# An adaLN block with linear attention and a gated MLP on one core: the columns of c first, other dummies, another order, the gate row at the joint, the last tile in two parts

## The chip, the core and the metric

The kernel runs on one core of a Trainium2 chip. Times are device microseconds (us) of one execution, and a kernel is judged by the median of several executions. The core has five instruction queues that are named here as in the profile: TensorE (PE, with its weight loads as PEld), VectorE (DVE), ScalarE (ACT), GpSimd (POOL) and SyncE (SP). SyncE only issues DMAs; ScalarE issues some as well.

## The reference

```python
mod = (silu(c) @ w_mod).reshape(c.shape[0], 6, 1, -1)
sa, ca, ga, sb, cb, gb = mod[:, 0], ..., mod[:, 5]
h = layernorm(x) * (1 + ca) + sa
x = x + ga * A(h)            # linear attention, 16 heads of 28
h = layernorm(x) * (1 + cb) + sb
x = x + gb * B(h)            # gated MLP with a spatial matrix
return x

def A(x):
    q, k, v = heads(x @ wqkv)
    phi_q = concat(softmax(q @ w_phi), softmax(-(q @ w_phi)))
    phi_k = concat(softmax(k @ w_phi), softmax(-(k @ w_phi)))
    kv, z = phi_k.T @ v, sum(phi_k)
    return merge((phi_q @ kv) / (phi_q @ z + 1e-6)) @ wo

def B(x):
    z = gelu(x @ w_in)
    z1, z2 = z[..., :896], layernorm(z[..., 896:])
    return (z1 * (w_sp @ z2 + b_sp)) @ w_out
```

x is [1, 2048, 448], c is [1, 448], w_sp is 2048 x 2048, w_in is 448 x 1792; everything is bf16. The six rows of mod depend on c alone.

## The kernel before

The 2048 tokens are 16 tiles of 128. The kernel is one long straight program: a string named ORDER lists some 890 steps, a loop runs through it and calls one small function for each step, and each function issues its instructions on its engine. Nothing is scheduled by a compiler: every engine executes its instructions in the order of the string, and waits at each for what it needs. A step is written `name:arguments@slot/engine`. The slot is the place in PSUM (A0, A1, A2 of two banks, B0, B1 of one) that the step's matmuls write, and a slot can be written again only when the last step that read it is done. The engine is V, S, G or Y for VectorE, ScalarE, GpSimd or SyncE; `ld:wk/Y` is the load of wk issued on SyncE's queue. The same words in another order are another schedule of the same arithmetic.

The steps that are spoken of, in the order of the program:

- `du:8` is eight dummy matmuls of 128x256 on a tile `zero` of zeros (L729, warm_ps). They compute nothing; they keep TensorE at work while the first data come in. `consts` fills `zero` on VectorE (L687).
- `ct` turns the row c into four columns by four tiny TensorE transposes (L740, ct_ps); `ce:1` to `ce:4` make silu of them (L747 to 753; ScalarE, then VectorE). `csA`, `ccA`, `csB`, `ccB` multiply these columns with sections of w_mod (L764, cf_ps, 16 one-column matmuls each); `esA`, `ecA`, `esB`, `ecB` read the products out on VectorE (L768, 771). sa and ca serve the first layer norm, sb and cb the second.
- `l1s`, `l1e`, `l1r`, `l1a` are the first layer norm: bn_stats of a tile on VectorE, moments, reciprocal root, and the normalised tile (L867, into xpad). `X` and `XE` transpose the first four tiles on TensorE (L880, xt_ps) and copy them out; `T1` transposes the others by a DMA on SyncE's queue (L872).
- `FT`, `ET`, `FS`, `PF`, `EP` fold w_phi and the scale into the weights Wk and Wq. `FT` transposes wk or wq.
- `kM`, `vM`, `qM` are the projections (L890, 898, 945), `kE`, `qE` the exponentials on ScalarE (L950 for q), `kS`, `kR`, `kP` the softmax of k, `kA` the accumulation of kv (L921), `KV`, `KZ` its reading. Up to here TensorE works on k and v; then the *joint*: kv is complete, and the stage of the attention's output begins.
- `gr:0` and `gr:1` make the gates ga and gb as 128 equal rows (L956, gr_ps, four matmuls of 448 columns each), `ge` copies them out on ScalarE, `wos` and `wts` multiply them into wo and w_out.
- `nM`, `nX`, `nC`, `nS`, `nT`, `nA`, `T2` are numerator, denominator, division and transpose of the attention's output; `wM` its product with wo (L1005, x_ps); `wR` adds the residual (L1012, f_x).
- `l2R`, `l2r`, `l2a`, `T3` are the second layer norm; `zM`, `zG`, `zQ`, `zR`, `zW`, `zN` the second half of z with its own layer norm (L1049 matmuls, L1017 squares, L1025 to 1035 moments, L1072 the normalised z2n); `yM`, `yG` the first half (L1078).
- `W` transposes w_sp by DMA. `tT`, `sS` form sums of blocks (L1102, L1109) so that seven products of blocks do for eight in w_sp @ z2; `P` are these products (L1124), `d` and `x` put them together (L1133 on VectorE, L1140 on GpSimd), `gM`, `gG` the last 128 columns, done plainly (L1145).
- `oM`, `oE`, `oD` are the output tile: seven matmuls of 448 columns (L1159, o_ps), the residual addition on VectorE (L1162) and the store (L1165).

How the string is read, and the loads on which the prediction speaks:

```python
"c": lambda q: q.dma_start(out=c_row[:], in_=c),
"wk": lambda q: load_rows(q, wk_raw[0:CB, :, 0:D], A_wqkv[:, D:2 * D]),
"win1": lambda q: load_rows(q, win_s[0:CB, 2:4], B_w_in[2 * CB:]),

def du(n, slot):
    wps = bank(slot, "warm_ps")
    for _ in range(n):
        nc.tensor.matmul(wps[:, 0, 0:256], lhsT=zero[:, 0:P], rhs=zero[:, 0:256], start=True, stop=True)
```

## Time and profile before

| what | value |
|---|---|
| runs (us) | 248.95, 249.26, 249.69; median 249.26 |
| profiled execution | 249.4 us, of which the span of the profile is 247.6 |
| instructions | 4188 |
| busy: PE, PEld, DVE, ACT, POOL | 97%, 51%, 74%, 42%, 47% of the span |
| HBM | 8.87 MB read, 1.84 MB written, 43 GB/s over the span |
| largest groups of matmuls | block products L1124 (29% of the chain that ended last), output L1159 (9%), z L1049 (7%) |

The profile is of one execution; times in it count from the start of its span, and 1.8 us of the execution lie outside it. An engine's busy share is the share of the span in which it executes. The chain that ended last is followed back from the last instruction to what released each step. In a row of a timeline, the bracket at the end gives the idle time of the engine just before the row and what ended it.

### The profile page before, as it was taken

The numbers are of one execution on the slowest core, as the hardware profiler recorded it, in microseconds if no ns is written. First come the engines' busy times: TensorE is split into PE (matmuls) and PEld (weight loads), VectorE is DVE, ScalarE is ACT, GpSimd is POOL, SyncE is SP. The second block draws the span as 40 slices with busy tenths as digits, with TensorE's granted clock in tenths as the row PEclk, the third lists the DMA queues.
The fourth block names the chain that finished last, engine by engine and source line by source line (L and its number), as shares of the span: only waits on it lengthen the run. The fifth ranks groups of instructions, "written<-read, shape, count | busy, mean of one in ns | idle before, by whom it ended". The sixth has DMA issues, their size and how long they took to land.

```text
span 247.6 us, 4188 instructions
## 1 busy us (share of the span) xinstructions
PE 240.5 (97%) x1533; PEld 126.8 (51%) x1533; DVE 182.5 (74%) x369; ACT 104.8 (42%) x217; POOL 116.3 (47%) x175
## 2 busy tenths in 40 slices
PE   8999999999999999999999999999999999999992
PEld 5865556675665564444444444444444444444451
DVE  4689998967999989686571997798976363645562
ACT  2488887836999896866897100000000000000000
POOL 3667997500387668987509000521129610124430
PEclk9999999999999999999999999999999999999998
DMA  7973849746235787989990999000001000101022
GB/s 178 293 217 102 193 86 177 194 113 178 51 72 110 127 162 136 163 158 176 179 177 0 162 181 173 0 1 0 3 0 37 0 0 3 56 0 37 21 95 65
DMA packets 68207, 25.22 MB, mean 102 GB/s; under 512 B 58129, under 2 KB 67602, under 8 KB 68178
## 3 DMA queue, kind: packets, MB, share of 16 engines
q1 hardware_dynamic: 66210, 22.57, 46.1%
q10 hardware_dynamic: 1968, 2.29, 3.3%
q8 instruction: 14, 0.23, 0.4%
q14 instruction: 15, 0.12, 0.2%
HBM read 8.87 MB, written 1.84 MB: 43 GB/s over the span
## 4 chain that ended last, share of the span: by engine, by line
PE 85%; POOL 6%; ACT 3%; DVE 2%; DMA 1%; issue 1%; POOLq 0%
PE g_ps L1124 29%; PE o_ps L1159 9%; PE z_ps L1049 7%; PE q_ps L945 6%; PE k_ps L890 5%; PE v_ps L898 5%; PE g_ps L1145 5%; PE z_ps L1078 4%; PE x_ps L1005 4%; PE kvacc L921 3%; PE warm_ps L729 3%; PE num L973 2%; POOL f_zv L1035 1%; DMA f_hT<-f_xpad 1%; DVE f_z2n L1072 1%
## 5 line engine op out<-in xcount | busy, mean ns | idle before, releaser
L1133 DVE TENSOR_TENSOR f_zb<-g_ps,f_zb 128x512 f32<-128x512 f32 (+1 forms) x31 | 20.5, 670 | 17.1 <-PE g_ps L1124 16.7
L1124 PEld LDWEIGHTS <-f_z2n 128*128 128x128 bf16 x192 | 18.8, 98 | 22.7 <-issue 0.3
L1140 POOL TENSOR_TENSOR f_z1T<-f_zb,f_z1T 128x512 bf16<-128x512 f32 (+1 forms) x11 | 12.0, 1102 | 33.6 <-DVE f_zb L1133 33.6
L1049 PE MATMUL z_ps<-f_ar,f_hT 112*128 112x448 bf16 (+1 forms) x128 | 26.6, 352 | 0.0
L1140 POOL TENSOR_TENSOR f_z1T<-f_Sx,f_z1T 128x512 bf16<-128x512 f32 x6 | 8.0, 1332 | 39.3 <-DVE f_Sx L1133 39.3
L1078 PE MATMUL z_ps<-f_hT,f_ar 112*128 112x512 bf16 x112 | 26.1, 379 | 0.0
L1159 PE MATMUL o_ps<-f_wout,f_z1T 128*128 128x448 bf16 x112 | 22.5, 352 | 0.0
L1124 PE MATMUL g_ps<-f_ar 128*128 128x512 bf16 x96 | 22.4, 379 | 0.0
L1081 ACT ACTIVATE f_z1T<-z_ps,f_zb 128x512 bf16<-128x512 f32 x28 | 18.2, 684 | 5.2 <-PE z_ps L1078 5.1
L950 ACT ACTIVATE f_Eq<-q_ps 112x1024 bf16<-112x1024 f32 x16 | 16.3, 1032 | 5.8 <-PE q_ps L945 5.8
L1049 PEld LDWEIGHTS <-f_hT 112*128 112x128 bf16 (+1 forms) x128 | 12.2, 97 | 11.6
L1078 PEld LDWEIGHTS <-f_ar 112*128 112x128 bf16 x112 | 11.0, 98 | 12.6
L893 ACT ACTIVATE f_E<-k_ps 128x448 bf16<-128x448 f32 x32 | 15.8, 555 | 3.8 <-PE k_ps L890 3.7
L989 DVE TENSOR_TENSOR f_ar<-num,f_w 128x896 bf16<-128x896 f32 x16 | 17.0, 1087 | 0.4
L904 DVE TENSOR_REDUCE f_ksum<-f_E 128x32 f32<-128x896 bf16 x16 | 16.9, 1064 | 0.5 <-ACT f_E L893 0.4
L1124 PE MATMUL g_ps<-f_Eq,f_z2n 128*128 128x512 bf16 x72 | 16.5, 379 | 0.0
L1159 PEld LDWEIGHTS <-f_z1T 128*128 128x128 bf16 x112 | 11.0, 98 | 10.7
L1053 ACT ACTIVATE f_zb<-z_ps 128x896 bf16<-128x896 f32 x16 | 14.6, 913 | 4.1 <-PE z_ps L1049 3.8
L1162 DVE TENSOR_TENSOR f_xpad<-o_ps,f_x 128x448 bf16<-128x448 f32 x16 | 9.9, 622 | 8.0 <-PE o_ps L1159 7.9
L945 PE MATMUL q_ps<-f_hT,f_Wq 113*128 113x512 bf16 (+1 forms) x64 | 15.0, 379 | 0.6 <-ACT f_Eq L950 0.6
L1124 PEld LDWEIGHTS <-f_ar 128*128 128x128 bf16 x96 | 9.4, 98 | 11.1 <-DVE f_ar L1102 0.2
L1005 PE MATMUL x_ps<-f_ar 112*128 112x448 bf16 x64 | 14.1, 352 | 0.3 <-DVE f_x L1012 0.3
(202 smaller groups left out, 473.1 us busy)
## 6 DMA issues: line engine op xcount, KB each, us to landing
out_dram<-f_xpad SPq DMA_DIRECT2D x16, 112.0 KB, 1.7
f_wm<-in_w_mod_dram SPq DMA_DIRECT2D x4, 406.0 KB, 5.1
f_x<-in_A_x_dram SPq DMA_DIRECT2D x2, 448.0 KB, 7.8
f_wmg<-in_w_mod_dram SPq DMA_DIRECT2D x2, 392.0 KB, 9.9
f_ar<-in_B_w_in_dram SPq DMA_DIRECT2D x1, 784.0 KB, 5.6
f_ar<-in_B_w_in_dram ACTq DMA_DIRECT2D x1, 784.0 KB, 5.4
f_wout<-in_B_w_out_dram ACTq DMA_DIRECT2D x1, 784.0 KB, 5.6
f_bsp<-in_B_b_sp_dram SPq DMA_DIRECT2D x1, 512.0 KB, 5.7
```

The lines of the kernel that those rows point to most:

```text
L904: nc.vector.tensor_reduce(out=ksum[:, i], in_=Er[i % NR][:].rearrange("p s (c f h) -> p (s c) h f", c=4, h=HP), axis=AX.X, op=ALU.add)
L945: nc.tensor.matmul(t[:, u, :], lhsT=Wq[0:KR[m], m, cc * CB:cc * CB + P], rhs=hT[0:KR[m], 4 * st:4 * st + 4, m, :], start=(m == 0), stop=(m ...
L950: nc.scalar.activation(out=Eq[st // 2][0:CB, 2 * c2:2 * c2 + 2, s, (st % 2) * 512:(st % 2 + 1) * 512], in_=ps["q" + str(n)][0:CB, :, :], f ...
L989: nc.vector.tensor_tensor(out=tr[i % 2][:], in0=numv(i)[:, :, :, 0:DH], in1=wr[i // 2 % 2][:, i % 2].unsqueeze(3).to_broadcast([P, 2, H, D ...
L1005: nc.tensor.matmul(t[:, 0, 0:D], lhsT=oT[0:CB, i % 4, cc, :], rhs=wo_s[0:CB, cc, :], start=(cc == 0 and not with_x), stop=(cc == KC - 1))
L1049: nc.tensor.matmul(t[:, hf, 0:D], lhsT=hT[0:KR[m], i, m, :], rhs=win_s[0:KR[m], m, FH + hf * D:FH + (hf + 1) * D], start=(m == 0), stop=(m ...
L1078: nc.tensor.matmul(t[:, 0, :], lhsT=win_s[0:CB, m, fc * P:(fc + 1) * P], rhs=hT[0:CB, 4 * st:4 * st + 4, m, :], start=(m == 0), stop=(m == ...
L1081: nc.scalar.activation(out=stage_b()["z1T"][:, fc, st * 512:(st + 1) * 512], in_=ps["y%d_%d" % (st, fc)][:, 0, :], func=ACT.Gelu_apprx_tan ...
L1124: nc.tensor.matmul(g, lhsT=sta[:, m, :], rhs=mov[:, m, :], start=(m == 0 and i in (1, 6, 7)), stop=(m == 7), skip_group_check=True)
L1133: nc.vector.tensor_tensor(out=o, in0=x, in1=y, op=ALU.add)
L1140: eng.tensor_tensor(out=z, in0=T[r][:, c0:c1], in1=z, op=ALU.mult)
L1159: nc.tensor.matmul(ps["o" + str(t)][:, 0, 0:D], lhsT=later["z1T"][:, FO[n], t * P:(t + 1) * P], rhs=wout_s[:, FO[n], :], start=(n == 0), s ...
```

## The change

Six edits are made together.

1. The load of c is the first DMA on ScalarE's queue, ahead of x1 and x0. Before, it was the second on SyncE's, behind wk.
2. `zero` is filled in its first 256 columns only, and this fill is VectorE's first instruction; before it was the third, over all 512 columns.
3. The dummies: 8 + 3 + 11 = 22 stood ahead of the columns of c, then 2 between the transposes of wk and 6 behind them. Now 18 stand ahead of the columns, 6 behind them, then the same 2, then 8. `csA` goes ahead of `X:0`.
4. From about the third v projection on the steps stand in another order, and several of them on another engine or slot. Among the loads win1 is now where x5 was on ScalarE's queue.
5. `gr:1` moves from the middle of the k and v projections to the joint, between the columns of cb and sb and the next q projection, into slot B0, and `ecB` (the reading of cb's columns, which stood in B0) ahead of the first `nC`.
6. The last output tile is made in two parts, columns 0 to 255 and 256 to 447, each with its own matmuls, addition and store (the new functions oP, oF, oG); the first store is issued on ScalarE's queue.

The diff, with the table cut to its start, the joint and its end:

```diff
 ORDER = """
-tbl du:8@B1 m2b/V ld:wk/Y du:3@A2 m2a/V du:11@A1 ld:c/Y ct@B0 ld:x1/S l1s:1 ld:x0/S l1s:0 m1/G ld:phi/Y ce:1 m3 FTk:1@B1 ...
-l1e:0,1/G FTk:0@A0 ld:wca/Y ce:3 ce:4 bd/V ld:x2/Y ld:wq/Y l1r:0,1 l1a:0/V du:6@A2 X:0@B0 ETk:0/S csA@A2 ETk:1/V ...
+tbl ld:c/S du:18@A1 m2b/V ld:wk/Y m2a/V ct@B0 ld:x1/S l1s:1 ld:x0/S l1s:0 m1/G ld:phi/Y ce:1 m3 du:6@A0 FTk:1@B1 ...
+l1e:0,1/G FTk:0@A0 ld:wca/Y ce:3 ce:4 bd/V ld:x2/Y ld:wq/Y l1r:0,1 l1a:0/V du:8@A1 csA@A2 X:0@B0 ETk:0/S ETk:1/V ...
...
-... nM:0@A1 qE:3 ld:wout/S nM:1@A0 nX:0 nX:1 qF:3 nC:0 csB@B0 W:0,1 ld:win1/Y nC:1 nS:0 ccB@B1 nT:0 qM:4@A2 qE:4 ...
+... nM:0@A1 nM:1@A0 nX:0 nX:1 ccB@B0 ecB nC:0 nC:1 nS:0 qF:3 nT:0 nA:0/V csB@B1 gr:1@B0 ge:1 qM:4@A2 qF:4 T2:0,1 ...
...
-... oM:14,0,7@B0 oM:15,0,7@B1 oE:14 oD:14/Y oE:15 oD:15/Y
+... oM:14,0,7@B0 oP:15,0,256@B1 oE:14 oD:14/Y oP:15,256,448@B0 oF:15,0,256 oG:15,0,256/S oF:15,256,448 oG:15,256,448/Y
...
     def consts():
+        nc.vector.memset(zero[:, 0:256], 0.0)
         nc.gpsimd.memset(wk_raw[0:CB, :, D:D + 16], 0.0)
         nc.gpsimd.memset(wq_raw[0:CB, :, D:D + 16], 0.0)
         nc.vector.memset(one1[:], 1.0)
         nc.vector.memset(warm[:], 0.0)
-        nc.vector.memset(zero[:], 0.0)
...
+    def oP(t, a, b, slot):
+        o = ps["op" + str(a)] = bank(slot, "o_ps")
+        for n in range(FC):
+            nc.tensor.matmul(o[:, 0, 0:b - a], lhsT=later["z1T"][:, FO[n], t * P:(t + 1) * P], rhs=wout_s[:, FO[n], a:b], start=(n == 0), stop=(n == FC - 1))
+
+    def oF(t, a, b):
+        nc.vector.tensor_tensor(out=later["ot"][t % 4][:, a:b], in0=ps["op" + str(a)][:, 0, 0:b - a], in1=x_sb[:, t, a:b], op=ALU.add)
+
+    def oG(t, a, b, eng):
+        eng.dma_start(out=outv[t][:, a:b], in_=later["ot"][t % 4][:, a:b])
```

What that does to single engines is shown at three places. First SyncE's queue at the program's start, before (f_c_row is the row c, f_wm the sections of w_mod):

```order
L645 DMA f_wk_raw<-in_A_wqkv_dram 112x4x448
L655 DMA f_c_row<-in_c_dram 1x448
L649 DMA f_phi<-in_A_w_phi_dram 112x4x28
L652 DMA f_wm_119<-in_w_mod_dram 112x4x464 x2
L658 DMA f_x<-in_A_x_dram 128x2x448
```

and ScalarE at the start of the changed kernel, where the same load now stands (its lines are 43 lower, since the string is shorter):

```order
L689 ACT_TABLE_LOAD
L689 ACTIVATE f_warm<-f_warm 128x1
L612 DMA f_c_row<-in_c_dram 1x448
L614 DMA f_x<-in_A_x_dram 128x448
L613 DMA f_x<-in_A_x_dram 128x448
L704 ACTIVATE f_e<-ct_ps 112x4
```

The load of c has left SyncE's queue, and x1 and x0 (L614, L613) stand one issue later on ScalarE's.

Second, VectorE at the joint, before (the first two rows read kv out; num is the numerators' PSUM, f_dn the denominators, f_cb the columns of cb):

```order
L931 TENSOR_TENSOR f_ar<-kvacc,f_mask 112x16x29 x2
L936 SCALAR_TENSOR_TENSOR f_ar<-kvacc,f_mask 112x16 x2
L980 TENSOR_TENSOR f_cr_101<-num,f_Sx 128x32 x2
L984 TENSOR_TENSOR f_dn_103<-f_cr_101 128x32
L985 RECIPROCAL f_dn_103<-f_dn_103 128x32
L986 TENSOR_TENSOR f_w_105<-f_Sx,f_dn_103 128x64
L989 TENSOR_TENSOR f_ar<-num,f_w_105 128x896
L995 TENSOR_TENSOR f_ar<-f_ar 128x4x112
L989 TENSOR_TENSOR f_ar<-num,f_w_105 128x896
L768 TENSOR_SCALAR f_cb_83<-cf_ps 112x4
```

and now:

```order
L888 TENSOR_TENSOR f_ar<-kvacc,f_mask 112x16x29 x2
L893 SCALAR_TENSOR_TENSOR f_ar<-kvacc,f_mask 112x16 x2
L725 TENSOR_SCALAR f_cb_83<-cf_ps 112x4
L937 TENSOR_TENSOR f_cr_101<-num,f_Sx 128x32 x2
L941 TENSOR_TENSOR f_dn_103<-f_cr_101 128x32
L942 RECIPROCAL f_dn_103<-f_dn_103 128x32
L943 TENSOR_TENSOR f_w_105<-f_Sx,f_dn_103 128x64
L946 TENSOR_TENSOR f_ar<-num,f_w_105 128x896
L952 TENSOR_TENSOR f_ar<-f_ar 128x4x112
```

The reading of cf_ps has moved from behind the division chain to a place ahead of it. On TensorE this piece is new behind the last column of the joint (gr_ps is gr:1; f_scb holds silu(c) in 128 equal columns, f_wmg the gate sections):

```order
L721 MATMUL cf_ps<-f_scol,f_wm_119 128x1
L913 LDWEIGHTS f_scb
L913 MATMUL gr_ps<-f_wmg,f_scb 128x448
L913 LDWEIGHTS f_scb
L913 MATMUL gr_ps<-f_wmg,f_scb 128x448
L913 LDWEIGHTS f_scb
L913 MATMUL gr_ps<-f_wmg,f_scb 128x448
L913 LDWEIGHTS f_scb
L913 MATMUL gr_ps<-f_wmg,f_scb 128x448
L902 LDWEIGHTS f_Wq
L902 MATMUL q_ps<-f_hT,f_Wq 128x512
```

Before, the columns (L764) were followed at once by the q projection (L945).

Third, VectorE around the residuals of tiles 10, 13 and 12, before (f_z2n is a normalised z2, f_zm and f_zv its moments, x_ps the product with wo):

```order
L1019 SCALAR_TENSOR_TENSOR f_ar,f_zs_93<-f_zb 128x896
L995 TENSOR_TENSOR f_ar<-f_ar 128x4x112
L1012 SCALAR_TENSOR_TENSOR f_x,f_s_88<-x_ps,f_x 128x448 x2
L1025 TENSOR_SCALAR f_zm<-f_zs_92 128x2
L1026 TENSOR_TENSOR f_sq<-f_zm 128x2
L1031 SCALAR_TENSOR_TENSOR f_zv<-f_zs_93,f_sq 128x2
L1032 TENSOR_SCALAR f_zv<-f_zv 128x2
L1072 TENSOR_SCALAR f_z2n<-f_zb,f_zm,f_zv 128x896
L1012 SCALAR_TENSOR_TENSOR f_x,f_s_88<-x_ps,f_x 128x448
```

and the same number of instructions in, now:

```order
L969 SCALAR_TENSOR_TENSOR f_x,f_s_88<-x_ps,f_x 128x448
L946 TENSOR_TENSOR f_ar<-num,f_w_106 128x896
L1029 TENSOR_SCALAR f_z2n<-f_zb,f_zm,f_zv 128x896
L952 TENSOR_TENSOR f_ar<-f_ar 128x4x112 x2
L969 SCALAR_TENSOR_TENSOR f_x,f_s_88<-x_ps,f_x 128x448 x2
L976 SCALAR_TENSOR_TENSOR f_ar,f_s_89<-f_x 128x448
L969 SCALAR_TENSOR_TENSOR f_x,f_s_88<-x_ps,f_x 128x448
```

The moments of z (L1025 to 1032) no longer stand between the residuals of this stretch, and z2n stands at other places among them.

More of the change, by code (lines that the diff above doesn't have):

```diff
@@ L494 @@
-W:0,6 kF:14 kE:15 kA:8@A0 kA:9@A0 kP:12/V kS:14 vM:11@A1 kF:15 kS:15 kA:10@A0 vM:14@B1 kR:14 vC:11 vM:15@B0 vC:14 vM:12@A2 vM:13@B1 vC:12 kA:11@A0 vC:13
-kP:13/G kA:12@A0 kR:15 kP:14/V kP:15/V wos:2/V kA:13@A0 kA:14@A0 vC:15 kA:15@A0 KV:0/V KV:1/V KZ:0 ld:win0/S qM:3@A2 KZ:1 nM:0@A1 qE:3 ld:wout/S nM:1@A0
-nX:0 nX:1 qF:3 nC:0 csB@B0 W:0,1 ld:win1/Y nC:1 nS:0 ccB@B1 nT:0 qM:4@A2 qE:4 nA:0/V nT:1 ecB nA:1/V wos:3/V qM:5@A1 nM:2@A0 qF:4 esB nX:2 nM:3@A2 nX:3
-FB@B1 wos:1/V nC:2 qE:5 T2:0,1 nC:3 nS:1 FBc/S qF:5 nT:2 nA:2/G wM:0/S@B0 nT:3 SHw:3@B1 wR:0/S SCw:0,3/S T2:1,2 nM:5@A1 nX:5 nM:4@A0 nC:5 nX:4 nC:4 nA:3/V
@@ L522 @@
[L522 to L525 removed]
+ORDER = """
@@ L1200, in fast_path @@
         "zM": zM, "zG": zG, "zQ": zQ, "zR": lambda a, b, eng: moments(a, b, eng, zs1, zs2, float(FH), zm, zv), "zW": lambda a, b: rpow(a, b, zv), "zN": zN,
-        "yM": yM, "yG": yG, "W": W, "gM": gM, "gG": gG, "tT": tT, "sS": sS, "gal": gal, "P": pM, "d": pD, "x": pX, "oM": oM, "oE": oE, "oD": oD, "guard": guard, "read": read, "hint": hint,
+        "yM": yM, "yG": yG, "W": W, "gM": gM, "gG": gG, "tT": tT, "sS": sS, "gal": gal, "P": pM, "d": pD, "x": pX, "oM": oM, "oE": oE, "oP": oP, "oF": oF, "oG": oG, "oD": oD, "guard": guard, "read": read, "hint": hint,
     }
```

41 lines of the change are left out of this document (1 added, 40 removed).

## The prediction

> **What bounds the kernel now.** I read the page's first part, then busy time of TensorE alone in stretches cut at its idle places, then the chain that ended last, then the timeline at each place. The first line is the page's; the others are the stretches (us, length, busy and matmuls, granted clock, DMA share, GB/s).
>
> ```profile
> PE 240.5 (97%) x1533; PEld 126.8 (51%) x1533; DVE 182.5 (74%) x369; ACT 104.8 (42%) x217; POOL 116.3 (47%) x175
> ...
> 0.00:1.23 1.23, 0.00 (x0) 1.00 0.00 0
> 1.23:54.00 52.77, 52.48 (x479) 1.00 0.75 172
> 54.00:58.00 4.00, 3.42 (x58) 1.00 0.93 263
> ...
> 243.20:247.59 4.39, 0.00 (x0) 0.78 0.20 63
> ```
>
> TensorE is busy 240.5 of 247.6 us. Of the 7.1 us of idle time 1.23 lie before its first matmul, 0.29 up to 54, 0.58 at the joint of the two stages (54 to 58) and 4.39 behind its last matmul; of the 0.6 that are left, two holes of 0.26 and 0.24 make up most (near 103 and 138, rows below). Nothing else matters unless it lets TensorE start earlier, takes matmuls away, closes one of the holes, opens a new one, or shortens the tail. The chain's rows (start, length, what) show what TensorE does first:
>
> ```profile
> 1.23 4.88 PE warm_ps L729 x22
> 6.11 0.46 PE ct_ps L740 x4
> ...
> 8.04 0.66 PE warm_ps L729 x6
> ...
> 9.55 0.26 PE xt_ps L880 x4
> ...
> 23.49 1.51 PE gr_ps L956 x8
> ```
>
> The dummies (warm_ps) lie on the chain: 22 of them at 4.88 / 22 = 222 ns, and six of them later at 0.66 / 6 = 110 ns. A dummy added here is therefore paid in full, with 0.22 or 0.11 us, unless the matmul behind it would have waited anyway.
>
> **The start.** Rows of the timeline (start, length, engine, line, what; idle time in brackets):
>
> ```profile
> 0.82 0.06 DVE L686 MEMSET f_warm<- 128x1 f32 x1
> ...
> 0.90 0.27 DVE L687 MEMSET f_zero<- 128x256 uint32 x1
> 0.92 0.38 ACTq L657 DMA_DIRECT2D f_x<-in_A_x_dram  x1
> ...
> 6.61 0.17 ACT L747 ACTIVATE f_e<-ct_ps 112x4 f32<-112x4 bf16 x1 [4.39 <-PE ct_ps L740]
> ...
> 8.65 0.71 POOL L867 TENSOR_SCALAR f_xpad<-f_x,f_nm,f_rs 128x448 bf16<-128x448 bf16 x1
> ```
>
> The fill of zero, which the dummies wait for, becomes VectorE's first instruction and half as long: between the 0.06 of a tiny fill and the 0.27 of the whole one, about 0.16. It ends near 0.94 instead of 1.17: **-0.23 us**, as everything behind it starts that much earlier. Eighteen dummies then end at 1.00 + 18 x 0.222 = 5.0, and the columns of c come a good 1.0 us earlier than at 6.11. That by itself gives little: the columns' first reader (0.17 on ScalarE) feeds a VectorE step that stands in the queue behind both bn_stats pairs of x, and what the next dummies and transposes wait for is not c. Behind the columns stand 6 + 2 + 8 dummies where 2 + 6 stood. Ahead of the first transposes of wk there are then 24 where there were 22, and ahead of wsa's columns (cf_ps) 34 where there were 30. Four dummies more cost 4 x 0.11 = 0.44 at the later rate and 4 x 0.222 = 0.89 at the earlier one. The first two fall about where the rate changes, the last two behind it: I take 0.18 + 0.22 = **+0.40**. From below: they cost nothing where TensorE would wait for x instead. x1 and x0 now stand behind c on ScalarE's queue, one issue of 0.38 later, and the second normalised tile, ready at 8.65 + 0.71 = 9.36, would come at up to 9.74, while its transposes (9.55 in the chain) come at about 9.7. So nothing is lost there beyond the dummies. Start and ramp together: +0.17, with ends -0.23 (the dummies free) and +0.66 (all at the earlier rate).
>
> The clock column reads 1.00 in the stretch from 1.23, although the same dummy takes twice as long there as later. [...]
>
> **The gate row at the joint.** gr:1 is four of the eight gr_ps matmuls (1.51 / 2 = 0.76 us). Before, it stands at 23.5 in an unbroken run of TensorE. The rows of the joint:
>
> ```profile
> 55.80 0.94 PE L764 MATMUL cf_ps<-f_scol,f_wm 112*128 112x1 bf16 x32
> ...
> 56.22 1.05 ACT L950 ACTIVATE f_Eq<-q_ps 112x1024 bf16<-112x1024 f32 x1
> ...
> 57.32 3.63 PE L945 MATMUL q_ps<-f_hT,f_Wq 113*128 113x512 bf16 x16 [0.58 <-ACT f_Eq L950]
> ...
> 59.92 0.15 DVE L768 TENSOR_SCALAR f_cb<-cf_ps 112x4 f32<-112x4 f32 x1
> ```
>
> Between the columns (end 56.74) and the next q matmuls (57.32, which need a PSUM slot that the second exponential still reads) TensorE idles 0.58. gr:1 takes 0.76 of work from the full stretch and puts it into this hole; what does not fit is 0.18. Net **-0.58 us**. Its slot B0 held the scale columns, so it must wait for the 0.15 read on VectorE, which stood at 59.92 and now goes ahead of the first nC. It is ready some 0.2 us after the columns of the scale, while the shift columns run. Behind it on VectorE the first division chain starts 0.15 later, which I take as covered: the q matmuls (3.63) stand between it and its reader. ScalarE's copy ge:1 goes behind the second exponential, where nobody waits for it. Ends: 0 (the hole only moves) and -0.58; I take the full value because the hole's length is set by ScalarE, whose two exponentials keep their place.
>
> **The other order.** The same matmuls, with other engines and places. The two late holes and what stood in front:
>
> ```profile
> 102.61 0.51 DVE L1072 TENSOR_SCALAR f_z2n<-f_zb,f_zm,f_zv 128x896 bf16<-128x896 bf16 x1 [1.96 <-POOL f_zv L1035]
> ...
> 103.04 0.62 DVE L1012 SCALAR_TENSOR_TENSOR f_x<-x_ps,f_x 128x448 bf16<-128x448 f32 x1
> ...
> 103.72 0.92 PE L1005 MATMUL x_ps<-f_ar 112*128 112x448 bf16 x4 [0.26 <-DVE f_x L1012]
> ...
> 130.11 2.12 POOL L1102 TENSOR_TENSOR f_ar<-f_z2n 128x1024 bf16<-128x1024 bf16 x1 [7.34 <-ACT f_ar L1017]
> ...
> 135.07 1.71 DVE L1072 TENSOR_SCALAR f_z2n<-f_zb,f_zm,f_zv 128x896 bf16<-128x896 bf16 x2 [6.42 <-POOL f_zv L1035]
> ...
> 137.87 1.04 PE L1145 MATMUL g_ps<-f_Eq,f_z2n 128*128 128x512 bf16 x4 [0.24 <-DVE f_z2n L1072]
> ```
>
> At 103 the residual of tile 10 stood behind a z2n that waited 1.96 us for GpSimd; in the new order it stands ahead of any such z2n. At 138 tile 12's z2n came after a 2.12 us subtraction on GpSimd; the new order gives that subtraction to VectorE, behind gG:1, and tile 12 to GpSimd. I count both holes as closed, **-0.50** (end 0 if each only moves).
>
> What is late next: the new order is as tight as the old. The first place is the transposed tiles 4 and 5 (T1:4,6).
>
> ```profile
> 19.51 0.39 ACTq L661 DMA_DIRECT2D f_x<-in_A_x_dram  x1
> ...
> 22.75 2.73 SPq L872 DMA_TRANSPOSE f_hT<-f_xpad  x2
> ...
> DMA to landing us min/median/max: 3.1/3.2/3.3
> ...
> 26.57 1.68 PE L890 MATMUL k_ps<-f_Wk,f_hT 113*128 113x448 bf16 x8
> ...
> f_ar<-in_B_w_in_dram ACTq DMA_DIRECT2D x1, 784.0 KB, 5.4
> ```
>
> They land at 22.75 + 3.3 = 26.05, and kM:5 reads them at 26.57; without gr:1 and with kA:0 (0.42) ahead of it, it comes at 26.23. That leaves 0.2 us, and win1, 784 KB and 5.4 us to landing, is now issued on ScalarE's queue where x5 (448 KB) was at 19.51, so its tail still moves when they do. A dozen such places have a few tenths to spare; I put **+0.30** for new holes, from 0 to the 1.08 that the old order's holes sum to.
>
> **The last tile.**
>
> ```profile
> 232.58 0.42 DVE L1133 TENSOR_TENSOR f_zb<-g_ps,f_zb 128x256 f32<-128x256 f32 x1 [0.51 <-PE g_ps L1124]
> ...
> 235.77 0.68 DVE L1133 TENSOR_TENSOR f_zb<-g_ps,f_zb 128x512 f32<-128x512 f32 x1
> ...
> 243.17 0.62 DVE L1162 TENSOR_TENSOR f_xpad<-o_ps,f_x 128x448 bf16<-128x448 f32 x1 [0.70 <-PE o_ps L1159]
> 243.83 0.43 SPq L1165 DMA_DIRECT2D out_dram<-f_xpad  x1
> ```
>
> The last addition is 448 columns, 0.62 us, and only then is the store issued. In two parts only the second addition (192 columns) is left behind the last matmul. By 0.42 for 256 and 0.68 for 512 columns a column costs 1.0 ns, so 192 cost about 0.36: **-0.26**. Seven matmuls of 256 columns (0.11 each, as a dummy's) and seven of 192 (about 0.08, in proportion) are 1.35 us, as the 1.32 before; the second part's slot is free when tile 14's 0.62 addition is done, which fits into the 0.77 of the first part. The first part's store goes out on ScalarE's queue, idle there, ahead of the second. Ends: 0 (14 weight loads instead of seven hold the matmuls up) and -0.35 (a smaller last store lands sooner too).
>
> **The sum.** +0.17 - 0.58 - 0.50 + 0.30 - 0.26 = -0.87 us. The profiled execution took 249.4 us (span 247.6 and 1.8 around it), so it would take 248.5; it stood 0.14 above the median of 249.26, so I forecast **248.4 us** as a median. Within 0.3% (0.75 us) this kernel cannot be told from no change, and -0.87 is only just beyond it.
>
> **Rivals.**
> *The new order has as many holes as the old* (0.30). The old one had 0.58 + 0.26 + 0.24 = 1.08. With +1.08 instead of +0.30 the sum is -0.09; with half of that and a dear ramp (+0.45) it is -0.35, which I take: 248.9 us, no change. For it speaks how short the spare times are; against it, that the old order ran from 1.23 to 54 with 0.29 us of idle time.
> *T1 lands late behind win1* (0.10): slower. Place: kM:5 at 26.2. If win1, issued where x5 was (19.5), lands at 24.9 and the transposes move nothing until then, they land 3.3 later, at 28.2, and TensorE waits 2.0: with the 0.30 taken off, 248.4 + 1.7 = 250.1 us. It decides from a landing at 27.4 on, which undoes the gain, and can be measured from 28.1. Against it: the bigger part of win1's bytes is in before the transposes begin.
> *The rate changes earlier* (0.10): 248.0 us. If half rate ends with the earlier first dummies and the four more are covered by waits for x, the ramp gives -0.23 instead of +0.17. For it, the first columns at 5.0; against it, that TensorE did not wait for x before. [...]
> *The numbers as forecast* (0.50): 247.9 to 248.8.
>
> **How the numbers follow.** Beyond -0.75 us (under 248.5) lie 0.7 of the likeliest case, the whole case of the rate and a tenth of the first rival: faster 0.48. Within: the rest of the likeliest (0.15), 0.25 of the first rival and a little of the second: 0.42. Slower 0.10. The range 247.8 to 249.5 goes from the ramp at its best, with the holes closed, to the first rival with the dear ramp; outside stay the late landing and rare sums.
>
> **What would show each step.** Right: first dummy at 1.0; no idle TensorE before the q matmuls behind the joint, with gr_ps there; no idle time near 103 and 138; a last addition of 0.36. Wrong: the second tile's transposes later than 10.2; a wait of k_ps for a DMA near 26; TensorE's idle time between 2 and 243 over 0.8 in the sum; a tail behind the last matmul still 4.4.

## The result, and the profile after

The changed kernel took 259.5 us as a median (257.43 to 260.21 in four runs) against 249.47 (the three runs given above and a fourth): it is 3.8% slower, ratio 1.0382 with a 95% interval of 1.0310 to 1.0454. The forecast was 248.4. The profiled execution took 259.04 us with a span of 257.2, so 9.6 us of span came on top. In the changed kernel all lines are 43 lower than before (L764 is L721).

First the stretches of TensorE alone, cut at the places where something happens (us, length, busy and matmuls, granted clock, DMA share, GB/s):

```profile
0.00:1.04 1.04, 0.00 (x0) 1.00 0.00 0
1.04:8.18 7.14, 7.08 (x54) 1.00 0.97 224
8.18:11.61 3.43, 1.68 (x30) 1.00 1.13 260
11.61:18.43 6.82, 6.82 (x73) 0.50 0.98 266
18.43:46.60 28.17, 28.17 (x222) 1.00 0.58 111
46.60:47.76 1.16, 0.01 (x2) 1.00 1.20 269
...
249.57:257.20 7.63, 0.00 (x1) 0.79 0.16 40
```

In the kernel before, the third of these stretches reads:

```profile
8.18:11.61 3.43, 3.43 (x80) 1.00 1.12 293
```

Where the kernel before was busy all the time, TensorE is now busy for 1.68 of 3.43 us, and the 6.82 us that follow are granted half the clock. A busy share of 100% in that row hides the loss: the four matmuls of a k projection take 1.70 us in it (at 14.44) and 0.93 behind it (at 20.94). And the stretch behind the last matmul is 7.6 us where it was 4.4.

The timeline of the start (as in the prediction) shows how the holes came about:

```profile
1.04 3.95 PE L686 MATMUL warm_ps<-f_zero 128*128 128x256 bf16 x18 [1.04 <-DVE f_warm L644]
1.08 0.55 ACTq L612 DMA_DIRECT2D f_c_row<-in_c_dram  x1
1.70 1.02 SPq L609 DMA_DIRECT2D f_wm<-in_w_mod_dram  x2
2.09 0.45 ACTq L613 DMA_DIRECT2D f_x<-in_A_x_dram  x1
4.92 0.36 PE L697 MATMUL ct_ps<-f_one,f_c_row 1*112 1x1 bf16 x4
...
7.47 0.63 DVE L813 BATCH_NORM_STATS2 f_st<-f_x 128x6 f32<-128x448 bf16 x1 [1.41 <-DMA f_x<-in_A_x_dram]
8.23 0.14 DVE L706 TENSOR_SCALAR f_e<-f_e 112x4 f32<-112x4 f32 x1
8.90 0.54 PE L721 MATMUL cf_ps<-f_scol,f_wm 112*128 112x1 bf16 x16 [0.72 <-DVE f_scol L710]
...
10.31 0.40 PE L837 MATMUL xt_ps<-f_ident,f_xpad 128*128 128x128 bf16 x4 [0.87 <-DVE f_xpad L824]
```

The rows of the kernel before for x0, the w_mod sections, the bn_stats of x0 and the step of silu behind it:

```profile
1.34 0.44 ACTq L656 DMA_DIRECT2D f_x<-in_A_x_dram  x1
1.98 1.01 SPq L652 DMA_DIRECT2D f_wm<-in_w_mod_dram  x2
5.54 0.59 DVE L856 BATCH_NORM_STATS2 f_st<-f_x 128x6 f32<-128x448 bf16 x1
6.81 0.17 DVE L749 TENSOR_SCALAR f_e<-f_e 112x4 f32<-112x4 f32 x1 [0.46 <-ACT f_e L747]
```

The columns of c are there at 4.92, 1.1 us earlier than before, and the 18 dummies ended in time. But x0 is issued at 2.09, now behind the first of the two w_mod sections, wsa, which is issued on SyncE's queue at 1.70 (before: 1.98, with x0 at 1.34). Issued behind it, x0 lands at 7.44 instead of 5.4: 0.75 of the 2.0 us are the later issue, the rest is a flight of 5.35 instead of 4.08 us. Its bn_stats waits until 7.47, and the next step of silu(c) (f_e) stands behind it on VectorE, so the columns that had come early are used 1.4 us later than before. TensorE waits 0.72 and 0.87 us and then gets the half clock. The third k projection, at 16.82 before (first row), starts at 20.94 (second row): 4.1 us lost.

```profile
16.82 0.92 PE L890 MATMUL k_ps<-f_Wk,f_hT 113*128 113x448 bf16 x4
20.94 0.93 PE L847 MATMUL k_ps<-f_Wk,f_hT 113*128 113x448 bf16 x4
```

An estimate from these figures comes to nearly the same: 0.44 for four dummies more, 1.36 for the holes (1.59, less 0.23 that the kernel before has at 11.88), 3.41 for 6.82 us at half clock, less 0.19 for the earlier first dummy and less 0.96 because full rate began at 4.78 and not at 6.69 (by the trace's clock records; half of the 1.91, as a dummy takes 222 ns before and 110 later), which is 4.06.

The other places, by the timeline: the joint (two rows), then the loads ahead of a transpose on SyncE's queue, and the three waits of TensorE for transposes:

```profile
61.32 0.92 PE L913 MATMUL gr_ps<-f_wmg,f_scb 112*128 112x448 bf16 x4
62.08 3.63 PE L902 MATMUL q_ps<-f_hT,f_Wq 113*128 113x512 bf16 x16
...
39.46 1.33 SPq L1043 DMA_TRANSPOSE f_wsp<-in_B_w_sp_dram  x1
40.88 0.54 SPq L609 DMA_DIRECT2D f_wm<-in_w_mod_dram  x1
41.52 5.08 SPq L829 DMA_TRANSPOSE f_hT<-f_xpad  x2
47.76 1.69 PE L847 MATMUL k_ps<-f_Wk,f_hT 113*128 113x448 bf16 x8 [1.15 <-DMA f_hT<-f_xpad]
70.52 0.93 PE L962 MATMUL x_ps<-f_ar 112*128 112x448 bf16 x4 [0.51 <-DMA f_ar<-f_ar]
88.10 1.04 PE L1035 MATMUL z_ps<-f_hT,f_ar 112*128 112x512 bf16 x4 [1.35 <-DMA f_hT<-f_xpad]
```

The joint has no hole any more, and the holes near 103 and 138 are gone. In their place stand three waits for DMA transposes, 3.01 us together. The first is for T1:12,14, which is now issued behind W:0,5 (f_wsp) and the section sb (f_wm). The chain that ended last has its flight as one piece:

```profile
40.09 1.42 POOL f_xpad L824 x2
41.52 6.19 DMA f_hT<-f_xpad
47.76 1.69 PE k_ps L847 x8
```

It takes 6.19 us; before, the same transposes were issued at 36.51 and had landed at 40.25.

The tail: the last addition is short, as planned, and yet the span goes on for 7 us more.

```profile
249.61 0.36 DVE L1130 TENSOR_TENSOR f_xpad<-o_ps,f_x 128x192 bf16<-128x192 f32 x1 [0.27 <-PE o_ps L1127]
250.00 0.33 SPq L1133 DMA_DIRECT2D out_dram<-f_xpad  x1
```

What follows are instructions that the timeline leaves out; the DRAIN among them stands at the end of each engine's part. From the trace's own records (us):

```
                          before    after
last matmul ends          243.14    249.57
last store landed         246.05    253.03
TensorE: last semaphore   245.31    252.94
TensorE: DRAIN            245.46    256.47
instruction fetch, 16 KB  242.23    249.89    (start)
the next one              246.01    253.49    (start; took 1.70 after)
end of the span           247.59    257.23
```

After, TensorE executes its last semaphore, and its next instruction, a DRAIN, follows only 3.5 us later, behind a fetch of instructions. The other engines wait for it: SyncE, the last of them, has its own DRAIN behind it at 253.76, and the next semaphore of any engine (GpSimd's) comes at 256.52.

The sum against the profile of before: +4.12 at the third k projection, +3.01 for the three waits, -1.08 for the old holes, and the last matmul is 6.43 later, so 0.38 are left for small pieces that I did not follow one by one (0.13 of it the last tile's 14 matmuls); the tail is 3.21 longer. Together these are the 9.64 by which the span grew.

### The profile page after: what moved, and what is told of

Its sections match the earlier page's. It is cut to its first block, busy times and chain, and to the rows that moved or that the text cites. A ratio compares the mean times of both kernels' runs of the same rounds, so it can differ in the third digit from the quotient of the medians.

```text
span 257.2 us, 4218 instructions
## 1 busy us (share of the span) xinstructions
PE 243.6 (95%) x1544; PEld 128.7 (50%) x1544; DVE 181.4 (71%) x363; ACT 109.7 (43%) x224; POOL 124.3 (48%) x173
## 4 chain that ended last, share of the span: by engine, by line
PE 73%; DVE 9%; POOL 7%; DMA 6%; issue 1%; ACT 0%; ACTq 0%; POOLq 0%
PE g_ps L1081 28%; PE z_ps L1035 9%; PE z_ps L1006 8%; PE o_ps L1116 8%; PE g_ps L1102 5%; DMA f_hT<-f_xpad 4%; DVE f_st L813 3%; PE x_ps L962 2%; PE k_ps L847 2%; DMA f_x<-in_A_x_dram 2%; PE q_ps L902 2%; DVE f_ksum L861 2%; POOL f_xpad L824 2%; PE v_ps L855 1%; PE num L930 1%; PE kvacc L878 1%
## 5 line engine op out<-in xcount | busy, mean ns | idle before, releaser
L1090 DVE TENSOR_TENSOR f_zb<-g_ps,f_zb 128x512 f32<-128x512 f32 (+1 forms) x31 | 20.6, 669 | 16.9 <-PE g_ps L1081 16.7
L1006 PE MATMUL z_ps<-f_ar,f_hT 112*128 112x448 bf16 (+1 forms) x128 | 26.0, 352 | 0.0
L1097 POOL TENSOR_TENSOR f_z1T<-f_Sx,f_z1T 128x512 bf16<-128x512 f32 x6 | 9.1, 1510 | 27.8 <-DVE f_Sx L1090 27.8
L1116 PE MATMUL o_ps<-f_wout,f_z1T 128*128 128x448 bf16 x105 | 21.2, 352 | 0.0
L946 DVE TENSOR_TENSOR f_ar<-num,f_w 128x896 bf16<-128x896 f32 x16 | 16.9, 1087 | 0.4
L847 PE MATMUL k_ps<-f_Wk,f_hT 113*128 113x448 bf16 (+1 forms) x64 | 15.6, 375 | 1.1 <-DMA f_hT<-f_xpad 1.1
L1116 PEld LDWEIGHTS <-f_z1T 128*128 128x128 bf16 x105 | 10.3, 98 | 10.0
```

Of the source, the lines that this page charges most:

```text
L847: nc.tensor.matmul(t[:, 0, 0:D], lhsT=hT[0:KR[m], i, m, :], rhs=Wk[0:KR[m], m, :], start=(m == 0), stop=(m == KC - 1))
L946: nc.vector.tensor_tensor(out=tr[i % 2][:], in0=numv(i)[:, :, :, 0:DH], in1=wr[i // 2 % 2][:, i % 2].unsqueeze(3).to_broadcast([P, 2, H, D ...
L1006: nc.tensor.matmul(t[:, hf, 0:D], lhsT=hT[0:KR[m], i, m, :], rhs=win_s[0:KR[m], m, FH + hf * D:FH + (hf + 1) * D], start=(m == 0), stop=(m ...
L1090: nc.vector.tensor_tensor(out=o, in0=x, in1=y, op=ALU.add)
L1097: eng.tensor_tensor(out=z, in0=T[r][:, c0:c1], in1=z, op=ALU.mult)
L1116: nc.tensor.matmul(ps["o" + str(t)][:, 0, 0:D], lhsT=later["z1T"][:, FO[n], t * P:(t + 1) * P], rhs=wout_s[:, FO[n], :], start=(n == 0), s ...
```

## Experiments

Times are medians; ratios are to the kernel before, run on the same chip in turn. "Tail" is the time from the end of the last matmul to the end of the span.

**The start.** Theory: x0 is issued behind wsa, and the holes that follow bring the half clock. Rivals: the new counts of dummies; c on ScalarE's queue wherever it stands.

```diff
-tbl ld:c/S du:18@A1 m2b/V ld:wk/Y m2a/V ct@B0 ...
+tbl du:18@A1 m2b/V ld:wk/Y m2a/V ld:c/Y ct@B0 ...
```

> The changed kernel with one edit: the load of c goes back to SyncE's queue behind wk. Theory (late x0): in the changed kernel x0 is issued at 2.09, behind the 416 KB of wsa, and lands at 7.44 instead of 5.41; the silu of c stands behind its bn_stats on VectorE, TensorE gets two holes (0.72 and 0.87) between 8 and 10.3, and the clock record falls to half from 11.6 to 18.4. With c on SyncE x0 should land by 5.7, no half rate after the first microseconds, third k projection near 17.1 instead of 20.94, and the time 3.5 to 5.5 us lower: 254 to 256 us. Rival (the dummies): 18 ahead of c and 6 behind shift the weights' transposes and csA; then x0 lands earlier but the half rate stays, 258 to 260 us.

256.47 us, ratio 1.0276 (1.0193 to 1.0358): 3.0 us less than the changed kernel, and 0.5 above the expected range. x0 landed at 6.05, no half clock after the first microseconds, and the third k projection came at 17.23, 3.7 us earlier. The dummies were untouched, so they were not the cause of the holes. (The time fell by less than those 3.7: TensorE waited 1.78 and 1.14 us for T1, where the changed kernel waits 1.15.)

The opposite edit, c first on ScalarE's queue in the old kernel and nothing else:

> The old kernel with one edit: the load of c is the first DMA on ScalarE's queue. Theory late x0: x0 lands near 7.4 instead of 5.4, its bn_stats and the silu behind it 2 us later, TensorE with holes of over 1 us before 10.5 and half rate for some 6.8 us: 253 to 255 us against 249.3. Rival (22 dummies ahead of c and 6 before the transposes still cover it, it takes both edits): 249 to 250.5 us.

252.53 us, ratio 1.0098 (1.0058 to 1.0139), just under the expected range. x0 landed at 7.41, with a hole of 2.76 and the half clock behind it:

```profile
10.27 0.40 PE L882 MATMUL xt_ps<-f_ident,f_xpad 128*128 128x128 bf16 x4 [2.76 <-DVE f_xpad L869]
...
10.88:17.71 6.83, 6.83 (x83) 0.50 1.09 282
```

The first row is of the timeline, the second of the stretches. Of ten runs, the three with a mean granted clock of 0.999 or more took 250.6 to 251.0 us, and the four with 0.983 to 0.986 took 253.2 to 254.1. The clock varies from run to run with the same code, and the runs with the lower clock took 2.2 to 3.5 us longer. The undisturbed runs lose 1.1 to 1.4 against the kernel before; how long their hole was isn't shown, since none of them was profiled. Moving one load of 896 bytes ahead of two others therefore cost 1.1 to 4.5 us.

Dummies in the holes, seven ahead of csA and nine ahead of the first transposes:

```diff
-du:8@A1 csA@A2 X:0@B0
+du:15@A1 csA@A2 du:9@A1 X:0@B0
```

> The changed kernel with 16 more dummies in the two holes of the start: 7 more ahead of csA and 9 between csA and the first transposes, 16 x 0.11 = 1.8 us of added work. Theory late x0 with the clock: what costs is the half rate from 11.6 to 18.4 that follows the holes (3.4 us), so filling them with work that computes nothing makes the kernel faster: the clock stays at full rate, third k projection near 17.9 to 18.3, 255 to 257 us. Rival (the holes' own length is the loss, 1.6 us, and the half rate has another cause): half rate stays, 259 to 260 us.

254.61 us, ratio 1.0200 (1.0131 to 1.0268): 4.9 us less than the changed kernel, by adding 1.8 us of work that computes nothing. The stretches that were 1.68 busy, then at half clock:

```profile
8.18:11.61 3.43, 3.43 (x52) 1.00 1.13 267
11.61:18.43 6.82, 6.58 (x110) 1.00 1.01 265
```

The third k projection came at 18.99, 1.95 earlier, though not at the 17.9 to 18.3 that I expected (in this run full rate began only at 7.04, against 4.78 in the profile of the changed kernel, which by an estimate, half of the difference, takes back 1.1). Of the rest, 3.1 us is the tail: 4.58 instead of 7.66, which belongs to the third group below.

Last, c on ScalarE's queue but behind x1 and x0:

> The changed kernel with c still on ScalarE's queue, but behind x1 and x0 instead of ahead of them. Theory late x0: what costs is not c's queue but that x0 is issued behind wsa (1.70). Now x0 is issued at 1.5 and should land at 5.6 to 6.1, the holes before 10.5 sum to under 0.6 us and there is no half rate; the third k projection at 16.9 to 17.4, 255 to 257 us (the late DRAIN stays). Rival (c on ScalarE's queue is the cause, in any place): x0 or c late, holes over 1 us, 258 to 260 us.

256.78 us, ratio 1.0304 (1.0253 to 1.0355). x0 landed at 5.60 as expected, but the hole had only changed its place:

```profile
6.11 0.36 PE L742 MATMUL ct_ps<-f_one,f_c_row 1*112 1x1 bf16 x4 [1.65 <-DMA f_c_row<-in_c_dram]
```

Now c was late, and 18 dummies did not cover it; the half clock came at 7.11 and lasted 3.41 us. For x0 it is therefore not the queue that counts, but whether it is issued behind the 406 KB of wsa: 0.2 to 0.4 us behind it, its 112 KB flew for 5.35 to 5.81 us in the four profiles where that was so, and for 4.04 to 4.55 elsewhere. With the 896 bytes of c it is another matter. By its semaphore it landed at 6.06, 4.04 us after its issue at 2.02; in the kernel before it took 4.01, in the changed kernel 3.41. It came 1.6 us later than in the changed kernel, and 0.94 of that is the later issue; that wsa held it up isn't shown. My expectation of 16.9 to 17.4 for the third k projection missed (18.94), since it looked at x0 alone.

**The order on SyncE's queue.** First the whole old start, so that the new order, the gate row and the two parts are left:

> The changed kernel with the whole start of the old one (c on SyncE, 22 dummies ahead of c, old fill of zero), so the new order, the gate row at the joint and the last tile in two parts alone. Theory late x0: the same as with c alone put back, within 0.6 us, and the third k projection at 16.8 to 17.0. What is then left above 249.3 belongs to the order and the tail. If the waits for transposes (1.15, 0.51, 1.35 us in the changed kernel) come from the new order by itself, 253 to 256 us; if they only follow from the late start, 249 to 251 us. Rival (the dummies are the cause, not c): this one is 4 us faster than the one with c alone put back.

252.66 us, ratio 1.0102 (1.0030 to 1.0173). That is 3.8 us less than with c alone put back, the sign that I had named for the dummies. The profiles place it elsewhere: the third k projection is only 0.53 earlier (16.70), the waits behind it are 1.5 us shorter and the tail is 1.85 shorter (5.00), which has to do with the number of instructions (below). TensorE still waits 1.39 us for T1:12,14 and 1.66 us for T3:2,4, so these two waits belong to the new order and not to the late start; the 0.51 in front of x_ps is gone with it. To this, the two loads behind the transposes:

```diff
-... kP:8/G W:0,5 kM:11@B0 kS:10 ld:wsb/Y kF:11 ... T1:12,14 kS:11 T1:14,16 ...
+... kP:8/G kM:11@B0 kS:10 kF:11 ... T1:12,14 kS:11 T1:14,16 W:0,5 ld:wsb/Y ...
```

> The changed kernel with the old start, and on SyncE's queue the loads W:0,5 and wsb moved behind the transposes T1:12,14 and T1:14,16, as in the old order. Theory (queue): in the new order T1:12,14 is issued behind wsb and lands 6.2 to 6.8 us after its issue (3.5 to 3.7 in the old order), and the k projection of tile 12 waits 1.4 us for it. With the loads behind it, it should land within 4 us and the wait be under 0.3: 251 to 251.7 us against 252.66 with the old start alone. Rival (other traffic or GpSimd's late xpad is the cause): the wait stays over 1 us and the time within 0.5 us of 252.66.

250.06 us, ratio 1.0027 (0.9996 to 1.0058), 2.6 us less, more than expected: SyncE's queue now reads

```profile
31.30 7.30 SPq L874 DMA_TRANSPOSE f_hT<-f_xpad  x4
38.66 2.11 SPq L1088 DMA_TRANSPOSE f_wsp<-in_B_w_sp_dram  x1
40.86 0.54 SPq L654 DMA_DIRECT2D f_wm<-in_w_mod_dram  x1
```

T1:12,14, issued at 35.97, landed at 39.48, and no k projection waits. Where 1.4 was the wait that was removed, the last matmul came 2.07 earlier in the profiles; 0.22 of the other 0.7 is a shorter wait for T3:2,4 (1.44 instead of 1.66), and 0.5 I can't place. Which of the two loads held the transposes up isn't separated.

**The end.** Theory: instructions come in blocks (the fetches in the table above are of 16 KB), and in the changed kernel a block of TensorE's ends between its last semaphore and its DRAIN. Rival: the two stores on two queues make the tail. The old kernel with the two parts alone:

> The old kernel with the last tile in two parts alone. By the prediction's term the last addition is 0.36 instead of 0.62: 0.26 us faster. Rival: the last store's issue is earlier by 0.3 but it lands no earlier relative to the last matmul (2.9 us after it in the old kernel, 3.4 to 3.5 in kernels with two parts), because three stores then end together: 0.2 to 0.6 us slower. Its stream is 14 instructions longer; if its end falls on a block boundary, the tail is 2 us longer besides.

251.05 us, ratio 1.0061 (1.0039 to 1.0083): slower, though the last matmul ends at 243.05 (before: 243.14) and the last addition takes 0.36 as forecast.

```profile
242.29 0.33 SPq L1167 DMA_DIRECT2D out_dram<-f_xpad  x1
242.40 0.42 DVE L1175 TENSOR_TENSOR f_xpad<-o_ps,f_x 128x256 bf16<-128x256 f32 x1
242.86 0.37 ACTq L1178 DMA_DIRECT2D out_dram<-f_xpad  x1
243.09 0.36 DVE L1175 TENSOR_TENSOR f_xpad<-o_ps,f_x 128x192 bf16<-128x192 f32 x1 [0.26 <-PE o_ps L1172]
243.48 0.33 SPq L1178 DMA_DIRECT2D out_dram<-f_xpad  x1
```

The last store is issued 0.35 earlier than before and lands 0.5 later, at 246.54; all three last stores land within 0.3 us of each other. In the ten kernels with two parts that were profiled, the last landing is 3.05 to 3.55 us behind the last matmul; in the seven with a whole tile it is 2.58 to 2.91. Besides, the execution lasted 2.4 to 2.9 us beyond the span in all seven runs, where the old kernel has 1.8 to 1.9.

Is that a matter of length? The same with 12 one-column matmuls more, hidden in the joint's hole:

> The old kernel with the last tile in two parts and 12 one-column matmuls more at the joint, so 38 instructions longer than the old one (24 longer than with two parts alone, which took 251.05 us). Theory (block boundary): with two parts alone the time outside the profile's span was 2.4 to 2.9 us instead of 1.8 to 1.9; with a longer stream it is back at 1.8 to 1.9, and the time 0.6 to 1.0 us lower, 250.0 to 250.5 us. What is then left above the old kernel is the two parts' own cost: stores land 3.4 to 3.5 us after the last matmul instead of 2.7 to 2.9, so +0.5. Rival (the two parts' store on ScalarE's queue makes the time outside the span long): 251 us and 2.4 to 2.9 again.

The time beyond the span was back at 1.8 to 2.0 in all nine runs, so it goes with the length of the stream and not with the stores. The time was no better: 251.22 us, ratio 1.0072 (1.0047 to 1.0098), since in this kernel T3:2,4 came late (a wait of 0.98 us that two parts alone did not have).

Eight dummies in the changed kernel with c on SyncE, in front of the k projection that waits:

```diff
-kA:7@A0 kM:12@B0
+kA:7@A0 du:8@B0 kM:12@B0
```

> The changed kernel with c back on SyncE and 8 dummies more, directly ahead of the k projection that waits 1.78 us for its transposes (so they cost nothing themselves). Theory (tail): in the changed kernel and with c put back TensorE's last DRAIN comes 2.4 to 3.4 us after its last semaphore, behind a 16 KB instruction fetch (253.49 in the changed kernel), because a block of its instructions ends between the two; where the stream was 8 shorter or 32 longer this did not occur. With 16 instructions more the DRAIN should follow its semaphore at once and the tail behind the last matmul be 4.4 to 5.0 instead of 6.85, so some 2 us faster than with c put back: 253.5 to 255 us. Rival (the stores on two queues, or the smaller last store, make the tail long): tail 6.8 again, 256 to 257 us.

252.05 us, ratio 1.0106 (1.0064 to 1.0147), 4.4 us less by adding work: the tail fell from 6.85 to 4.67, with the DRAIN 0.15 us behind its semaphore. The last matmul came 2.24 earlier as well: the waits for T1 and T2 (1.78, 1.14 and 0.51) were 0.29 and 0.29 in this execution, and the dummies took 0.88.

Then the length alone, 22 instructions on the old kernel:

> The old kernel with 11 matmuls of one column more, which compute nothing and lie in the hole of 0.58 us at the joint (a one-column matmul takes 0.03 us there), so 22 instructions more on TensorE and nothing else. Theory (block boundary): with the stream 22 longer, as in the changed kernel, TensorE's last DRAIN comes 2.4 to 3.4 us behind its last semaphore, and the kernel is 1.5 to 3 us slower: 250.8 to 252.3 us. Rival (the late DRAIN has to do with the stores or the new order): no change, 249.0 to 249.6 us.

250.55 us, ratio 1.0040 (1.0015 to 1.0065). A miss: no late DRAIN (246.48, semaphore 246.33; tail 4.11). The loss is a wait of 1.27 us for T3:2,4. So 22 was not the number that matters. By TensorE's records the changed kernel is not 22 but 21 instructions longer than the old one (11 dummies and matmuls with their weight loads, one semaphore fewer). If the boundary lies exactly between semaphore and DRAIN, one instruction more must move it ahead of the semaphore, where the stores' flight hides the fetch. So, one dummy in the changed kernel:

```diff
-kA:7@A0 kM:12@B0
+kA:7@A0 du:1@B0 kM:12@B0
```

> The changed kernel with a single dummy more (two instructions on TensorE), in the place where it waits over 1 us for transposes. Theory (block boundary, between two instructions): the changed kernel's stream is 21 instructions longer than the old one's and its boundary lies exactly between the last semaphore and the DRAIN; 22 longer showed no late DRAIN. So one dummy more moves it ahead of the semaphore, where the fetch runs while the stores fly: DRAIN right behind the semaphore, tail behind the last matmul under 5.2 instead of 7.66 us, and about 2.4 us faster: 256.3 to 257.8 us. Rival (the late DRAIN belongs to the changed kernel's stores or order, whatever the length): tail 7 us or more, 259 to 260 us.

255.25 us, ratio 1.0214 (1.0179 to 1.0249). The tail is 5.02 instead of 7.66, the semaphore at 253.66, the DRAIN at 253.80. A single dummy takes the 2.6 us away. (The median fell by 4.3, more than that. In the profiled execution, the slowest of the four, the third k projection came 1.87 earlier, without half clock at the start, but the last matmul 0.69 later, since a wait of 1.99 us and a half clock followed at 44 to 51. The run of 253.58 us had the full clock, but was not profiled.)

**The joint, the fill, and a faster version.** gr:1 at the joint of the old kernel:

> The old kernel with gr:1 at the joint alone (with ecB ahead of the first nC, cb's columns in B0, sb's in B1). Theory: the hole of 0.58 ahead of the q projection behind the joint is filled, as the changed kernel showed with no wait there: 0.5 to 0.6 us faster, 248.8 to 249.1 us against 249.57. Rival (the hole only moves: what was covered by 0.58 of slack waits elsewhere): within 0.2 us of the old kernel.

248.89 us, ratio 0.9978 (0.9959 to 0.9998). The joint is without a hole:

```profile
55.61 0.94 PE L766 MATMUL cf_ps<-f_scol,f_wm 112*128 112x1 bf16 x32
56.41 0.92 PE L958 MATMUL gr_ps<-f_wmg,f_scb 112*128 112x448 bf16 x4
57.17 3.63 PE L947 MATMUL q_ps<-f_hT,f_Wq 113*128 113x512 bf16 x16
```

The gain lies between 0.05 and 1.0 us and holds the -0.58 of the forecast. (In the profiles the last matmul comes only 0.10 earlier, but full rate began at 7.24 instead of 6.69, which by an estimate, half of the difference, costs 0.28.) To this, the fill of zero first:

> The old kernel with gr:1 at the joint and the fill of zero first, nothing else. Theory: gate alone 248.89 us, the fill 0.2 us less: 248.5 to 248.8 us. Rival (the earlier first dummy only lengthens the row of dummies' wait for the columns of c, which land at 5.2 to 5.4): 248.8 to 249.0 us.

249.12 us, ratio 0.9991 (0.9969 to 1.0013): no gain from the fill is shown. The dummies start at 1.04 instead of 1.23, but x1 and x0 are issued at 1.08 and 1.50 instead of 0.92 and 1.34, because ScalarE's first activation, which stands ahead of them in its queue, waits for the tiny fill; that now ends at 1.04 instead of 0.88. The hole ahead of the first transposes was 1.25 us, with the half clock from 11.35 to 14.76. This profile is of the slowest of the twelve runs, 251.76 us, which also waited 1.39 us for T3:2,4; the median run need not have had either.

The new order with its three faults mended (T1 ahead of the loads, the last tile whole, T3:2,4 issued as two of one tile), behind the old start with the new fill:

> The new order and the gate row at the joint, with the old start (but the fill of zero first), T1:12,14 and T1:14,16 ahead of W:0,5 and wsb, the last tile whole, and the transposes T3:2,4 issued as two of one tile each, the first as soon as its tile is ready. Theory: against the same without the last three (250.06 us) the whole tile gives 0.6 outside the span and 0.5 inside, the fill 0.2, and the wait of 1.44 us for T3:2,4 falls under 0.5: 247 to 248.4 us, faster than both kernels. Rival (the wait for T3 only moves, or the issue on SyncE's queue gets dearer by a fourth of a DMA): 248.5 to 249.3 us.

248.45 us, ratio 0.9954 (0.9927 to 0.9981), faster than both kernels. The wait for T3 is gone; the half clock was there in this profile, after a hole of 1.08 us:

```profile
7.88:11.30 3.42, 2.60 (x68) 1.00 1.12 280
11.30:14.71 3.41, 3.41 (x24) 0.50 1.12 324
```

With the old fill:

> The fastest version so far (new order and gate at the joint, whole last tile, T1 ahead of W:0,5 and wsb, T3:2,4 as two) with the old fill of zero. Theory: the fill ahead of the tiny one delays ScalarE's first instruction, and with it the issue of x1 and x0, by 0.16 us, while the dummies start 0.19 earlier; x0 then lands 0.3 later, the hole ahead of the first transposes grows from 0.4 to 0.7 us to 1.1 to 1.25, and at 1.1 or more the half rate follows. With the old fill the hole is 0.4 to 0.7, no half rate: 247.6 to 248.3 us. Rival (the fill's 0.19 counts in full): 248.5 to 248.8 us.

248.38 us, ratio 0.9957 (0.9939 to 0.9975). In the profile no hole at the first transposes and no half clock, TensorE idle for 0.3 up to 54 and not at all at the joint:

```profile
1.23:54.00 52.77, 52.47 (x478) 1.00 0.86 194
54.00:58.00 4.00, 4.00 (x61) 1.00 0.01 3
```

The medians of these two are alike, so neither the gain nor the loss by the fill shows. Of twelve runs, five with the early fill had a granted clock of 0.992 or less and took 249.0 to 251.1 us; with the old fill one of twelve did. That the fill makes the half clock more frequent isn't shown by this: the two ran on different chips, and the old kernel, which has the old fill, had such a clock in 8 of 34 runs on the first and in 3 of 17 on the second.

## Why the prediction was wrong

*The start (forecast +0.17, measured +4.1 in the profile).* This step failed: "x1 and x0 now stand behind c on ScalarE's queue, one issue of 0.38 later ... So nothing is lost there beyond the dummies." I counted the place on ScalarE's queue and not the place among all transfers in flight. The load that left SyncE's queue let wsa move up, and x0 moved down behind it: 0.75 later in the issue, 2.0 later in the landing. I had seen that silu's VectorE step stands behind both bn_stats pairs, and drew from it only that c's early arrival gives little, not that a late x0 would hold c. And two holes of 1.6 us in all cost 3.4 us more by the clock, a term that the sum did not have.

*New holes of the order (forecast +0.30, measured 3.01).* The term was mis-sized by ten. I named T1 as the place, but the wrong tiles and the wrong load: win1 landed at 26.63 and T1:4,6 was issued at 26.88, with no wait. I had also read its issue wrongly: in the string it stands ahead of the fourth k projection, where x5 stood behind it, and with the old start it was issued at 16.91, not at 19.5. What I did not cost is that two loads moved ahead of T1:12,14 on SyncE's queue. The wait for T3:2,4, the longest of the three, has no explanation; with the transposes issued as two it was gone.

*The joint (-0.58) and the late holes (-0.50).* Right as far as the changed kernel goes: there is no wait at these places, and gr:1 at the joint alone is faster by 0.2%. The late holes were given no run of their own, and they are not closed for good: with the 16 dummies more at the start, TensorE waited 0.94 us at 140.9, again with g_ps behind a z2n, now GpSimd's.

*The last tile (-0.26).* The addition was sized right (0.36), but a shorter last addition and a smaller last store (48 KB instead of 112) are not an earlier landing: with the two parts alone it came 0.5 later. *The tail* as a whole was no item of my sum, which, but for the last addition, put it at no change without a reason; measured it is +3.21, and the late DRAIN, 2.6 us of it, depends on how many instructions TensorE has.

*The fill (-0.23).* The first dummy came at 1.04 as forecast. That everything behind it starts as much earlier was wrong: what the start waits for is x, whose issue the same edit delayed by 0.16.

*The rivals.* None was it. T1 late was the nearest, at 0.10 and 250.1 us. The rate did change earlier, at 4.78 instead of 6.69, as the rival of 0.10 had it, but its gain was lost in the holes behind. The signs listed as wrong did show: the second tile's transposes at 11.22 against the 10.2 named, and a k projection that waits for a DMA (at 46.6, not 26).

## What to carry to other kernels

When a load changes its queue, list all DMA issues of all queues by their time, before and after, with their sizes: here a load of 112 KB that fell behind one of 406 KB landed within 0.7 us of it, and what stood behind its reader on the engine was late too. At a start without slack the holes have a second price: by the clock, 1.1 to 2.8 us of them cost 1.7 to 3.4 more in the five profiles where half rate followed at the start, and in the one kernel where dummies filled them, these were cheaper than the holes (1.8 us of dummies, and the third k projection 1.95 earlier). And when a change at the very end costs microseconds that no store or addition explains, add one harmless instruction and measure again: here a single dummy took 2.6 us off the tail.
